# Every second store of the transformed blocks issued from ScalarE's queue instead of SyncE's

## Chip, core and metric

One core of a Trainium2 chip. The metric is the device time of one execution in microseconds, as the median of several runs. Engines are named as in the profile: PE is TensorE (matmuls), PEld its weight loads, DVE is VectorE, ACT is ScalarE, POOL is GpSimd, SP is SyncE. A q behind the name (SPq, ACTq) is the engine's queue, its sequencer.

## What is computed

The kernel computes `x + s * g` for one sequence of L = 2048 rows of D = 512 columns. With `xn` the layer norm of `x`, `g` is a SwiGLU feed-forward of width 1792 with a further silu on its output, and `s` is a state-space convolution with 128 states for each column:

```python
K = jnp.einsum("dn,dnl,dn->dl", Cc, P, dB).real          # P = exp(dt*A*l), l = 0..L-1
Kf = rfft2(pad(K, L)); Uf = rfft2(pad(xn^T, L))
s = irfft2(Uf * Kf)[..., :L]^T + xn * Dskip
g = silu((silu(xn @ w_gate) * (xn @ w_up)) @ w_down)
return x + s * g
```

## The kernel before

The feed-forward is done on TensorE in fp16 with split operands: gate and up halves at line 717 (24 matmuls of 128x256 to a half), down products at line 760 (128x512). The convolution is a transform in stages, written as small f32 matmuls between the feed-forward's. For the convolution kernel K, ACT makes sines and cosines in PSUM (lines 1129 to 1131), DVE multiplies them with amplitudes (lines 1149 to 1157), PE sums over states (line 1181), and `kg_s1` does the first transform stage for 64 columns at a time: matmuls at line 1214 into four PSUM banks, copies out of them by ACT and DVE (line 1221) into a block of 128x2048 floats, an addition of the skip term by DVE (line 1227), and two stores of the block's partition halves, 64 partitions each, to the DRAM array `ak_d` (line 1229). That happens eight times, between 180 and 431 us. Each store moves 512 KB in pieces of 256 bytes.

The second stage (`s2_load`, `s2_prod`, `s2_inv`) loads `ak_d` and the transformed input `ax_d` back (line 464), transforms both (lines 1267 and 1275), multiplies them (DVE at lines 1293 and 1295, POOL at 1297 and 1298), goes back a stage (line 1320, with copies and sums at 1328 to 1330) and stores to `bs_d` (line 1332). `final` loads that and ends with the product with `g` and the sum with `x`.

Nothing waits for an order found while running. Every piece of work is a task, made by `add(engine, planned duration, function, ...)` with the buffers that it reads and writes. A table of numbers, `LIST`, gives the order of all 1989 tasks; each engine does its own in that order. A second table, `PLACES`, gives each SBUF buffer its address in one arena. Both tables are the same before and after. The rest is worked out by `Plan.run`, which goes through the tasks with a clock for each engine and uses the planned times for two things:

- The PSUM banks. When a task first touches a PSUM buffer, it gets the bank that is free earliest by the planned clock (`p0` to `p7`). In the program, a matmul into a bank waits for the bank's last readers.
- Dummy matmuls. `keep_warm` looks for planned gaps on PE. Where they sum to 1.0 us or more within 3.4 us, it fills each with multiplications of a constant by itself (line 1487, 128x512 bf16) into a bank that is free by the plan:

```python
if max(idle(a) for a in (s, s - WARM_SPAN / 2, e - WARM_SPAN)) < WARM_IDLE:
    continue
...
n = int((e - s - 0.2) * WARM_SHARE / WARM_DUR)
```

So a change of a task's engine or planned duration moves no task, but may move banks and dummies behind it. In before, all 35 dummies stand in the first 14 us.

Of the kernel before, what the change touches and what calls it, by code (L numbers as in the profile page):

```python
# [134 lines left out]
class Plan:  # L135
# [19 lines left out]
    def add(self, eng, dur, fn, rd=(), wr=(), up=(), pr=0.0, c=5, dma=0.0, root=False, port=None, f32=0, slack=0.0, ahead=None):  # L155

        t = Task()
        t.eng, t.dur, t.fn, t.pr, t.due, t.root, t.seq, t.dma = eng, dur, fn, (c, pr), pr, root, len(self.tasks), dma
        t.after = None
        t.f32, t.slack, t.ahead = f32, slack, W["ah"] if ahead is None else ahead
        t.port = eng == "POOL" if port is None else port
        deps = set()
        for b in rd:
            deps.update(b.full)
            deps.update(b.part)
        for b in up:  # L170
            deps.update(b.full)
            deps.update(b.reads)
        for b in wr:
            deps.update(b.full)
            deps.update(b.part)
            deps.update(b.reads)
        for b in rd:
            b.reads.append(t)
        for b in up:
            b.part.append(t)  # L180
        for b in wr:
            b.full.append(t)
        t.bufs = list(dict.fromkeys(b for b in (*rd, *wr, *up) if b.kind))
        for b in t.bufs:
            b.left += 1
        t.deps = deps
        t.succ = []
        self.tasks.append(t)
        return t
# [191 lines left out]
def kernel(  # L381
# [7 lines left out]
    nc = tc.nc  # L389
    V, S, G, T = nc.vector, nc.scalar, nc.gpsimd, nc.tensor  # L390
    sy = nc.sync
# [13 lines left out]
    ak_d = dram.tile([32, 2, 64, D], F32, name="ak_d")  # L405
# [37 lines left out]
    add = pl.add  # L443
    bufs = []

    def buf(name, size, group=None, cap=None):
        b = pl.buf(name, size, group, cap)
        bufs.append(b)
        return b

    def bank(name, *kinds):
        b = pl.bank(name, *(kinds or ("p",)))
        bufs.append(b)
        return b
# [3 lines left out]
    def key(name):  # L458
        if name not in K:
            K[name] = pl.key(name)  # L460
        return K[name]
# [522 lines left out]
    def k_target(ch):  # L984
        return W["k0"] + W["ks"] * ch / 8 + bend("bk", ch / D)
# [202 lines left out]
    def kg_s1(i):  # L1188

        pr = k_target(i * 32 + 24)  # L1190
        kp, kh = kps.pop(i)
        khs[i] = kh
        half = lambda t, k: t.rearrange("p (e k b) -> p k b e", k=2, b=32)[:, k]
        lo, hi = (lambda: kh.f32().rearrange("p (k b e) -> p k b e", k=2, e=8)[:, 0]), (lambda: kh.f32().rearrange("p (k b e) -> p k b e", k=2, e=8)[:, 1])

        def even_odd():
            V.tensor_tensor(hi(), lo(), half(kp.t, 1), op=ALU.subtract)
            V.tensor_tensor(lo(), lo(), half(kp.t, 1), op=ALU.add)
        add("ACT", 0.38, lambda: S.copy(lo(), half(kp.t, 0)), rd=[kp], wr=[kh], c=2, pr=pr)
        add("DVE", 0.87, even_odd, rd=[kp], wr=[kh], c=2, pr=pr)  # L1200
        q, s_ = divmod(i, 2)
        if not s_:
            return
        two = [khs.pop(i - 1), khs.pop(i)]
        ka = [bank(f"ka{i}{h}") for h in range(4)]
        b = buf(f"akb{q}", 8192, "akb", int(W["c_akb"] + 0.5))

        def mm():
            for v in range(2):
                for h in range(4):  # L1210
                    u_ = (h // 2 + v) % 2
                    r = slice(h * 32, h * 32 + 32)
                    for k in range(2):
                        T.matmul(ka[h].t[k * 64:k * 64 + 64, u_ * 256:(u_ + 1) * 256], f1k_t[r, k * 64:(k + 1) * 64],  # L1214
                                 two[v].f32()[r, k * 256:(k + 1) * 256], start=True, stop=True, tile_position=(h * 32, k * 64))
        add("PE", 1.0, mm, rd=[*two, key("f1k")], wr=ka, up=[b], c=2, pr=pr, f32=3, slack=1.0)
        for h in range(4):
            def ev(e, h=h):
                o = b.f32().rearrange("p (s u y e j) -> p u y s e j", u=2, y=2, e=8, j=2)
                for u_ in range(2):  # L1220
                    e(o[:, u_, (h // 2 + u_) % 2, :, :, h % 2], ka[h].t[:, u_ * 256:(u_ + 1) * 256].rearrange("p (s e) -> p s e", e=8))
            if h % 2:
                add("DVE", 0.76, lambda ev=ev: ev(V.tensor_copy), rd=[ka[h]], up=[b], c=2, pr=pr)
            else:
                add("ACT", 0.76, lambda ev=ev: ev(S.copy), rd=[ka[h]], up=[b], c=2, pr=pr)
        t0 = lambda: b.f32()[:, 31 * 64:32 * 64]
        add("DVE", 0.2, lambda: V.tensor_tensor(t0(), t0(), dsk[:, q * 64:q * 64 + 64], op=ALU.add), rd=[key(f"dsk{k}") for k in range(2)], wr=[b], c=2, pr=pr, port=True)
        for k in range(2):
            add("SP", 0.52, lambda k=k: sy.dma_start(ak_d.rearrange("g r s d -> (g r) s d")[:, k * 32:k * 32 + 32, q * 64:q * 64 + 64],
                                                     b.f32().rearrange("p (s d) -> p s d", d=64)[k * 64:k * 64 + 64]),  # L1230
                rd=[b], up=[key(f"ak{q // 4}")], c=0, dma=2.8)

# [226 lines left out]
    for pos, (b, c) in enumerate(seq):  # L1459
        while pos >= lead(pos) and 2 * NB * NC - len(downs) < 2 * (pos - lead(pos)) + 2:  # L1460
            d = downs.pop(0)
# [4 lines left out]
    for m in range(D // GT):  # L1466
        kg_tables(m)
        for g in range(m * RT, m * RT + RT):
            kg_trig(g)
            kg_prod(g)  # L1470
            kg_mm(g)
            if g % CB == CB - 1:
                kg_s1(g // CB)
# [61 lines left out]
```

## Time and profile before

| what | value |
|---|---|
| median of 3 runs | 579.1 us (578.53 to 579.45) |
| the profiled execution, its own time | 578.55 us |
| its span, first to last instruction | 576.8 us |
| PE / DVE / ACT / POOL busy | 98% / 76% / 58% / 57% of the span |
| mean granted PE clock | 1.000 |
| share of the DMA engines' time, SP's queue / ACT's queue | 55.5% / 1.5% |

A page of the profile gives busy times, the chain of work that ended last, and groups of equal instructions. A row of a timeline has the start in us, the duration in us, engine, line, operation, `out<-in`, shapes and the count; in brackets stand the idle time of the engine just before it and what ended that. A row of a table by stretch has the stretch, its length, then for PE, PEld, DVE, ACT and POOL the busy time and the count of instructions, then the granted PE clock, the DMA engines' busy share and GB/s. Buffer numbers are left out in rows of the profile: `p` is any PSUM bank, `arena` any SBUF buffer. Which bank is meant is read from the program's order.

### The profile page before, as it was taken

How to read it: one execution, taken by the hardware profiler on the slowest of the kernel's cores; microseconds unless marked ns; L12 is line 12 of the kernel's file. 1: busy time of each engine (PE TensorE's matmuls, PEld its weight loads, DVE VectorE, ACT ScalarE, POOL GpSimd, SP SyncE). 2: the span in 40 equal slices, each digit the busy share in tenths (PEclk: the TensorE clock that was granted, in tenths of full speed). 3: DMA queues.
4: the chain of work that ended last, by engine and by line, in shares of the span. 5: the costliest groups of instructions: out<-in, count | busy, mean ns of one | idle time of the engine just before them, and what ended most of it. 6: DMA issues, size and time to landing. Idle time of an engine off the chain costs nothing.

```text
span 576.8 us, 18270 instructions
## 1 busy us (share of the span) xinstructions
PE 565.2 (98%) x7570; PEld 405.9 (70%) x7570; DVE 440.9 (76%) x1006; ACT 334.7 (58%) x686; POOL 327.1 (57%) x301
## 2 busy tenths in 40 slices
PE   7999999999999999999999999999999999999996
PEld 3788896564886588757867688765766674678765
DVE  5988889846788998988887899977978765643533
ACT  5988667646767266777777778746752323231111
POOL 0144352299998168629998789997516152520041
PEclk9999999999999999999999999999999999999999
DMA  8888722251003171058005452697879987998997
GB/s 249 237 260 265 225 74 74 49 174 67 29 2 85 29 174 47 2 110 275 22 1 126 97 149 74 149 212 181 270 230 248 287 281 218 258 306 234 233 256 203
DMA packets 113155, 93.17 MB, mean 162 GB/s; under 512 B 51184, under 2 KB 97648, under 8 KB 113072
## 3 DMA queue, kind: packets, MB, share of 16 engines
q1 hardware_dynamic: 110432, 89.61, 55.5%
q10 hardware_dynamic: 2640, 2.39, 1.5%
q8 instruction: 59, 0.97, 0.7%
q14 instruction: 24, 0.20, 0.1%
HBM read 55.94 MB, written 32.90 MB: 154 GB/s over the span
## 4 chain that ended last, share of the span: by engine, by line
PE 93%; DMA 2%; SPq 2%; DVE 1%; issue 1%; ACT 0%; DVEq 0%
PE p L717 50%; PE p L760 24%; PE p L1181 5%; PE p L1267 3%; PE p L568 2%; PE p L1275 2%; PE p L1365 2%; PE p L1320 2%; PE p L769 2%; PE p L1214 2%; DMA arena<-bs_d 1%; DMA arena<-in_A_u_dram 1%; SPq L464 1%; PE p L830 1%; SPq L485 1%
## 5 line engine op out<-in xcount | busy, mean ns | idle before, releaser
L717 PE MATMUL p<-arena,wu 128*128 128x256 f16 x1344 | 154.6, 273 | 0.0
L717 PE MATMUL p<-arena,wg 128*128 128x256 f16 x1344 | 154.5, 273 | 0.0
L717 PEld LDWEIGHTS <-wg 128*128 128x128 f16 x1344 | 130.5, 98 | 21.4 <-issue 2.8
L717 PEld LDWEIGHTS <-wu 128*128 128x128 f16 x1344 | 130.2, 98 | 20.2 <-issue 3.7
L760 PE MATMUL p<-wd,arena 128*128 128x512 f16 x630 | 143.2, 379 | 0.0
L760 PEld LDWEIGHTS <-arena 128*128 128x128 f16 x630 | 59.7, 98 | 71.8 <-issue 6.1
L1114 POOL TENSOR_TENSOR arena<-arena 128x1536 f32<-128x1536 f32 x32 | 90.6, 2839 | 22.0 <-DVE arena L850 8.3
L739 ACT ACTIVATE arena<-p,inv 128x512 f32<-128x512 f32 x56 | 37.7, 685 | 65.9 <-PE p L717 62.5
L741 DVE SCALAR_TENSOR_TENSOR p<-p,shc,arena 128x512 f32<-128x512 f32 x56 | 42.0, 756 | 41.9 <-PE p L717 33.3
L1106 POOL TENSOR_TENSOR arena<-arena 128x1024 int32<-128x1024 int32 x32 | 62.4, 1955 | 20.0 <-DVE arena L532 7.8
L743 ACT CAST arena<-p 128x512 f16<-128x512 f32 x56 | 32.6, 586 | 38.4 <-DVE p L741 31.9
L1149 DVE TENSOR_TENSOR arena<-arena,p 128x512 f32<-128x512 f32 x64 | 43.6, 681 | 6.3 <-POOL arena L1047 2.5
L1129 ACT ACTIVATE p<-arena 128x512 f32<-128x512 int32 x64 | 38.5, 606 | 12.9 <-POOL arena L1106 8.3
L1396 POOL TENSOR_TENSOR arena<-arena 128x512 f32<-128x512 f32 x12 | 15.0, 1269 | 49.3 <-DMA arena<-in_A_u_dram 21.6
L1130 ACT ACTIVATE p<-p,halfpi 128x512 f32<-128x512 f32 x64 | 41.9, 662 | 1.2
L744 DVE TENSOR_TENSOR arena<-p,arena 128x512 f16<-128x512 f32 x56 | 37.5, 683 | 6.0 <-ACT arena L743 5.9
L1131 ACT ACTIVATE p<-arena 128x512 f32<-128x512 int32 x64 | 38.0, 604 | 6.9 <-POOL arena L1106 4.2
L1298 POOL TENSOR_TENSOR arena<-arena 128x512 f32<-128x512 f32 x16 | 20.3, 1274 | 30.7 <-DVE arena L1295 26.2
L1297 POOL TENSOR_TENSOR arena<-arena 128x512 f32<-128x512 f32 x16 | 20.4, 1276 | 25.4 <-issue 15.0
L1181 PEld LDWEIGHTS p<-arena 128*32 128x32 f32 x2048 | 29.4, 110 | 5.4 <-issue 2.9
L1181 PE MATMUL p<-arena 128*32 128x64 f32 x2048 | 32.3, 220 | 0.0
L1293 DVE TENSOR_TENSOR arena<-p,arena 128x512 f32<-128x512 f32 x32 | 21.1, 685 | 13.9 <-PE p L1275 7.7
(198 smaller groups left out, 815.5 us busy)
## 6 DMA issues: line engine op xcount, KB each, us to landing
ax_d<-arena SPq DMA_DIRECT2D x32, 256.0 KB, 2.9
ak_d<-arena SPq DMA_DIRECT2D x16, 512.0 KB, 5.6
arena<-ak_d SPq DMA_DIRECT2D x16, 512.0 KB, 4.6
arena<-ax_d SPq DMA_DIRECT2D x16, 512.0 KB, 5.1
bs_d<-arena SPq DMA_DIRECT2D x32, 256.0 KB, 3.8
arena<-in_A_u_dram SPq DMA_DIRECT2D x62, 128.0 KB, 3.9
arena<-in_B_w_down_dram SPq DMA_DIRECT2D x14, 512.0 KB, 5.1
arena<-bs_d SPq DMA_DIRECT2D x12, 512.0 KB, 6.7
```

The source lines that it names most:

```text
L717: T.matmul(pg.t[:, i * 256:(i + 1) * 256].rearrange("p (a t) -> p a t", a=2), w[:, wl, d, i * P:(i + 1) * P], x[:, :, xl, d, :], start=(k ...
L739: add("ACT", 0.69, lambda: S.activation(sg.f32(), pg.t, AF.Silu, scale=inv[:, c, 0:1]), rd=[pg], wr=[sg], c=1, pr=e)
L741: add("DVE", 0.75, lambda: V.scalar_tensor_tensor(pu.t, pu.t, shc[:, c:c + 1], sg.f32(), op0=ALU.mult, op1=ALU.mult), rd=[sg], wr=[pu], c= ...
L744: add("DVE", 0.7, lambda: V.tensor_tensor(hh.view(F16)[:, 512:1024], pu.t, hh.view(F16)[:, 0:512], op=ALU.subtract), rd=[pu], wr=[hh], c=1 ...
L760: T.matmul(z.t, h[:, hl, i * 256 + t * P:i * 256 + (t + 1) * P], w[:, wl, i], start=(c == 0 and i == 0 and k == 0), stop=(c == NC - 1 and ...
L1106: G.tensor_tensor(a, h_[:, :, :, None].to_broadcast([P, 2 * GT, 4, 8]), l_[:, :, None, :].to_broadcast([P, 2 * GT, 4, 8]), op=ALU.add)
L1114: G.tensor_tensor(e, p_[:, :, :, None].to_broadcast([P, 3 * GT, 4, 8]), q_[:, :, None, :].to_broadcast([P, 3 * GT, 4, 8]), op=ALU.mult)
L1129: add("ACT", 0.62, lambda: S.activation(tc_.t, a(), AF.Abs, scale=SIN_SCALE), rd=[an], wr=[tc_], pr=pr)
L1130: add("ACT", 0.7, lambda: S.activation(tc_.t, tc_.t, AF.Sin, bias=halfpi, scale=-1.0), rd=[key("ones")], wr=[tc_], c=4, pr=pr)
L1131: add("ACT", 0.62, lambda: S.activation(ts.t, a(), AF.Sin, scale=SIN_SCALE), rd=[an], wr=[ts], pr=pr + 0.2)
L1149: V.tensor_tensor(o[:, :, 0:64].rearrange("p d (s j) -> p d s j", s=2), e[:, :, 0:64].rearrange("p d (s j) -> p d s j", s=2), t[:, :, None ...
L1181: T.matmul(kt[h * 32:(h + 1) * 32, (r * GD + dd) // 4], o[:, ri, dd + h, 64:96], o[:, ri, dd + h, 0:64], start=(ri == 0), stop=(ri == 1), ...
```

## The change

The second of the two stores, partitions 64 to 127 of the block, is issued by ACT instead of SP. It stays at the same place of `LIST`.

```diff
         for k in range(2):
-            add("SP", 0.52, lambda k=k: sy.dma_start(ak_d.rearrange("g r s d -> (g r) s d")[:, k * 32:k * 32 + 32, q * 64:q * 64 + 64],
+            add(("SP", "ACT")[k], 0.52, lambda k=k: (sy, nc.scalar)[k].dma_start(ak_d.rearrange("g r s d -> (g r) s d")[:, k * 32:k * 32 + 32, q * 64:q * 64 + 64],
                                                      b.f32().rearrange("p (s d) -> p s d", d=64)[k * 64:k * 64 + 64]),
                 rd=[b], up=[key(f"ak{q // 4}")], c=0, dma=2.8)
```

SP's queue has eight issues fewer and ACT's eight more; every other instruction of these two keeps its order. On ACT the eight stand, in order: behind the copy L1199 at 185 us of before's trace; behind two L1130 at 204; behind the first of four copies L573 at 257; behind L1130 at 308; behind L739 at 339; behind the last of four copies L1284 at 390; behind the third of four copies L1330 at 401; behind the cast L743 at 434. POOL's program is the same. On PE and DVE the order of work is the same; banks differ from 197 us on, and ten rows are new on PE. Three places, with the banks' numbers (`p7_106` is bank p7):

PE, between two gate halves L717, which start at 407 us in before's trace. In before the second half follows the first at once. The changed program has these rows, of which five pairs L1487 are new:

```order
L717 MATMUL p1_100<-arena_98,wg_75 128x256
L1487 LDWEIGHTS ones_90
L1487 MATMUL p7_106<-ones_90 128x512
...
L1487 LDWEIGHTS ones_90
L1487 MATMUL p7_106<-ones_90 128x512
L717 LDWEIGHTS wg_75
L717 MATMUL p4_103<-arena_98,wg_75 128x256
```

The planner has come to see a gap there and fills it with five dummy matmuls into p7.

DVE, at 371 to 375 us in before's trace, the products L1149 and L1151 that read the cosines out of a bank; before first:

```order
L1149 TENSOR_TENSOR arena_98<-arena_98,p7_106 128x8x64
L1151 TENSOR_TENSOR arena_98<-arena_98,p7_106 128x8x32
L741 SCALAR_TENSOR_TENSOR p3_102<-p3_102,shc_86,arena_98 128x512
L1149 TENSOR_TENSOR arena_98<-arena_98,p6_105 128x8x64
L1151 TENSOR_TENSOR arena_98<-arena_98,p6_105 128x8x32
```

And the same five rows of the changed program:

```order
L1149 TENSOR_TENSOR arena_98<-arena_98,p3_102 128x8x64
L1151 TENSOR_TENSOR arena_98<-arena_98,p3_102 128x8x32
L741 SCALAR_TENSOR_TENSOR p5_104<-p5_104,shc_86,arena_98 128x512
L1149 TENSOR_TENSOR arena_98<-arena_98,p7_106 128x8x64
L1151 TENSOR_TENSOR arena_98<-arena_98,p7_106 128x8x32
```

The last pair, at 374.04 and 374.64 us, reads p7 instead of p6. The gate half L717 that PE starts at 374.48 us writes p7 in both programs.

DVE and PE, at 440 to 443 us in before's trace: DVE's products of the second stage, and PE's next transform L1267, which alternates between two banks. Before, DVE and then PE:

```order
L1295 TENSOR_TENSOR arena_98<-p5_104,arena_98 128x512
L1293 TENSOR_TENSOR arena_98<-p0_99,arena_98 128x512
L1293 TENSOR_TENSOR arena_98<-p4_103,arena_98 128x512
L1295 TENSOR_TENSOR arena_98<-p1_100,arena_98 128x512
```
```order
L1320 MATMUL p2_101<-arena_98 32x256 x4
L1267 MATMUL p0_99<-arena_98 32x256
L1267 MATMUL p5_104<-arena_98 32x256
```

And in the changed program:

```order
L1295 TENSOR_TENSOR arena_98<-p5_104,arena_98 128x512
L1293 TENSOR_TENSOR arena_98<-p0_99,arena_98 128x512
L1293 TENSOR_TENSOR arena_98<-p4_103,arena_98 128x512
L1295 TENSOR_TENSOR arena_98<-p2_101,arena_98 128x512
```
```order
L1320 MATMUL p1_100<-arena_98 32x256 x4
L1267 MATMUL p0_99<-arena_98 32x256
L1267 MATMUL p2_101<-arena_98 32x256
```

The second bank of L1267 was that of the first L1295, p5; it is that of the last L1295 now, p2.

## The prediction

> **What bounds the kernel now.** I read the page first: busy times, then the chain that ended last.
>
> ```profile
> PE 565.2 (98%) x7570; PEld 405.9 (70%) x7570; DVE 440.9 (76%) x1006; ACT 334.7 (58%) x686; POOL 327.1 (57%) x301
> ...
> PE 93%; DMA 2%; SPq 2%; DVE 1%; issue 1%; ACT 0%; DVEq 0%
> ```
>
> TensorE is busy for 98% of the span and makes 93% of the chain; ScalarE has no visible share of it and SP's queue 2%. Any time that this change is to save or to cost must show on TensorE, as idle time that goes or comes, or as work that is added. Next I looked for TensorE's idle time, with the busy times by stretch (second number of each row: PE busy, of the stretch's length).
>
> ```profile
> 380.00:400.00 20.00, 19.16 (x413) 10.31 (x412) 14.15 (x32) 8.92 (x20) 15.96 (x16) 1.00 0.70 193
> 420.00:430.00 10.00, 8.91 (x355) 5.45 (x354) 6.82 (x14) 5.81 (x14) 1.96 (x2) 1.00 0.69 228
> 440.00:460.00 20.00, 19.81 (x393) 12.32 (x377) 16.84 (x36) 6.97 (x19) 9.39 (x8) 1.00 0.90 277
> 540.00:560.00 20.00, 19.62 (x154) 13.63 (x150) 10.42 (x17) 2.44 (x4) 5.94 (x5) 1.00 0.99 254
> ```
>
> From 20 us to 560 us these four are the only stretches with idle time: 0.84 + 1.09 + 0.19 + 0.38 = 2.50 us. All else there is TensorE running without a break, at a granted clock of 1.00. So at most 2.5 us can be won before the last outputs, and each microsecond put into TensorE's queue, by an instruction or by a wait, is a microsecond of the end.
>
> The stores themselves, from the answer for line 1229 (durations in ns on SP's queue, then issue to landing in us), and the last pair of them in SP's timeline:
>
> ```profile
> L1229 SPq DMA_DIRECT2D ak_d<-arena x16: 580/640/3182, 179.7 to 430.6; - x16
> ...
> DMA to landing us min/median/max: 4.6/5.6/7.6
> ```
> ```profile
> 429.93 3.81 SPq L1229 DMA_DIRECT2D ak_d<-arena  x2
> ```
>
> A first store takes SP about 0.6 us; a second behind it up to 3.18 us.
>
> **The change, part by part.** *SP's queue* loses eight issues of 0.6 to 3.18 us, 5 to 25 us of its time. Its 2% of the chain lies at the end (the chain's last loads), over 100 us behind the last of these stores, and TensorE idles only 0.38 us there. I count the relief as 0; its bound is priced under the rivals.
>
> *ScalarE's queue* gains eight issues. Its DMA instructions hold the queue as SP's do, and none of that form stands on ACT before. The nearest rows are SP's: 0.6 us for a store that stands alone, 3.18 us at most; I take 0.6, since the first store of the pair is in another queue. Whether ACT would wait for the block's data shows at the closest place, the fourth pair: SP could issue from 307.31 us, so the block was ready by then, and ACT's instruction ahead of the new store began at 307.83.
>
> ```profile
> 307.31 2.31 SPq L1229 DMA_DIRECT2D ak_d<-arena  x2
> ```
> ```profile
> 307.83 0.66 ACT L1130 ACTIVATE p<-p,halfpi 128x512 f32<-128x512 f32 x1
> ```
>
> In the other seven ACT comes 0.9 us or more behind SP's first issue, so ACT only pays the issue. Behind the first, second, third, sixth and eighth store ACT next idles by itself:
>
> ```profile
> 187.29 0.60 ACT L1129 ACTIVATE p<-arena 128x512 f32<-128x512 int32 x1 [2.14 <-POOL arena L1106]
> ```
> ```profile
> 207.79 1.12 ACT L1131 ACTIVATE p<-arena 128x512 f32<-128x512 int32 x2 [2.43 <-POOL arena L1106]
> ```
> ```profile
> 260.98 0.58 ACT L838 ACTIVATE arena<-p 128x64 int32<-128x64 f32 x4 [1.29 <-PE p L830]
> ```
> ```profile
> 392.65 0.60 ACT L1131 ACTIVATE p<-arena 128x512 f32<-128x512 int32 x1 [1.78 <-DVE arena L1293]
> ```
> ```profile
> 436.19 0.69 ACT L739 ACTIVATE arena<-p,inv 128x512 f32<-128x512 f32 x1 [1.92 <-PE p L717]
> ```
>
> Each idle time (the number in brackets) is over 0.6 us, so the issue ends in it. The fourth (about 308 us) and fifth (about 340 us) lie in busy stretches of ACT; what stands behind them comes 0.6 us late until ACT's next gap. Since ACT is 58% busy and not on the chain, I count all eight as 0, with the seventh as the risk:
>
> ```profile
> 400.92 0.92 ACT L1330 COPY arena<-p 128x256 f32<-128x256 f32 x3 [0.20 <-PE p L1320]
> ...
> 406.32 0.69 ACT L784 ACTIVATE arena<-p,zsc 128x512 f32<-128x512 f32 x1 [0.75 <-DMA ak_d<-arena]
> ```
>
> Here L784 already waits for the landing of the seventh pair (its output lies where the pair's block lay). The second store now stands behind the three copies L1330, so it is issued at about 401.9 us and lands 4.6 to 7.6 us later, at 406.5 to 409.5: L784 and everything behind it on ACT come 0.2 to 3.2 us late.
>
> *What moves beside it.* The planner counts each second store as time of ACT instead of SP, and from the shifted times it draws other PSUM banks and other gaps to fill. Instruction order is the same otherwise; three things fall on TensorE.
>
> First, five dummy matmuls (line 1487) now stand between two gate halves L717. The trace of before has no gap there:
>
> ```profile
> 407.21 5.40 PE L717 MATMUL p<-arena,wg 128*128 128x256 f16 x48
> ```
> ```profile
> 251.19 5.18 PE p L760 x24
> ```
>
> The 48 matmuls of the two halves run without a break, from 407.21. A matmul of the dummies' size (128x512) costs 5.18/24 = 0.216 us in the second row, from the chain in order of time; five are 1.08 us, with nothing to lie beside. The dummies themselves ran at the kernel's start:
>
> ```profile
> 1.05 7.30 PE L1487 MATMUL p<-ones 128*128 128x512 bf16 x21 [1.05 <-DVE halfpi L470]
> ```
>
> These are 7.30/21 = 0.35 us each, which bounds the term at 1.74 us. I take 1.08: the row in the middle of the stream is nearer to the place.
>
> Second, at 374.48 us a gate half L717 writes bank p7. In before, p7 was free by then; now p7 is the bank that VectorE's L1149 and L1151 read last (p6 in before).
>
> ```profile
> 374.48 1.25 PE L717 MATMUL p<-arena,wg 128*128 128x256 f16 x10
> ```
> ```profile
> 374.04 0.69 DVE L1149 TENSOR_TENSOR arena<-arena,p 128x512 f32<-128x512 f32 x1 [1.13 <-POOL arena L1114]
> 374.64 0.41 DVE L1151 TENSOR_TENSOR arena<-arena,p 128x256 f32<-128x256 f32 x1
> ```
>
> L1151 ends at 375.05, 0.57 us after TensorE was ready; with the hand-over TensorE stands about 0.6 us. L1149 was itself held up by GpSimd's L1114 (the 1.13 in its row), so the term can shrink to 0 if TensorE is later for another reason.
>
> Third, at 441.79 us the transform L1267 alternates between two banks: p0 and p5 in before, p0 and p2 now. TensorE's and VectorE's rows there:
>
> ```profile
> 441.79 1.10 PE L1267 MATMUL p<-arena 64*32 64x256 f32 x32 [0.19 <-DVE arena L1293]
> ```
> ```profile
> 440.45 0.69 DVE L1295 TENSOR_TENSOR arena<-p,arena 128x512 f32<-128x512 f32 x1 [1.13 <-PE p L1275]
> 441.06 1.28 DVE L1293 TENSOR_TENSOR arena<-p,arena 128x512 f32<-128x512 f32 x2
> 442.25 0.68 DVE L1295 TENSOR_TENSOR arena<-p,arena 128x512 f32<-128x512 f32 x1
> ```
>
> VectorE reads p5 with the first L1295 (done 441.14) and the second bank's tenant, p1 in before and p2 now, with the last (done 442.93). The first L1267 matmul starts at 441.79 as before; the second must wait until 442.93 plus a hand-over of 0.05 (L1293 on p0 ended at 441.74, L1267 began at 441.79), so 442.98 instead of 441.85: 1.13 us. VectorE's four instructions were started by TensorE's own L1275, so this wait moves along with TensorE, and earlier delays do not eat it.
>
> Sum: 1.08 + 0.60 + 1.13 = 2.81 us. The profiled execution took 578.55 us (span 576.8, 1.75 around it), so it would take 581.36; the median of the runs shown is 579.1, so I forecast 579.1 + 2.8 = **581.9 us**.
>
> The Trainium skill's page "DMA: Bandwidth & Descriptors", section "Rules for kernel authors", speaks against this change: two transfers of disjoint partition halves share the same 16 engines whichever engine issues them, so spreading them gains no bandwidth and saves only the sequencer's issue time. By that rule alone the sum would be 0 and the time 579.1; it says nothing of banks and dummies.
>
> **The rivals.** *Only the queue changes (0.15).* The bank waits do not come, because TensorE arrives later than in this trace, or the dummies fall into a stall that it has anyway. For it: the second term has a reader that is late for a reason of its own. Against it: the third is tied to TensorE's own time. With the dummies alone the time is 579.1 + 1.08 = 580.2, without them 579.1. The page just named gives the latter; whether the stores gain bandwidth from a second queue, no row of before shows.
>
> *The freed queue wins (0.05).* Faster is possible if spreading the stores takes away TensorE's stalls that the profile puts down to nothing visible. There are two in the chain, the first of them while SP issues the sixth pair:
>
> ```profile
> 384.41 3.52 SPq L1229 DMA_DIRECT2D ak_d<-arena  x2
> ```
> ```profile
> 385.73 0.84 issue
> ...
> 426.03 0.72 issue
> ```
>
> If all 2.50 us of idle time went and neither bank wait came, 1.08 for the dummies would still be added: 579.1 − 1.42 = 577.7. It decides only when at least 2.24 of the 2.50 us go (1.08 + 1.16), since 0.2% is 1.16 us, about what a measurement of this kernel can tell from no change. Against it: 0.56 us of that idle time is TensorE waiting for other engines and not for a queue, the 0.19 of the third term and this:
>
> ```profile
> 424.96 1.07 PE L1214 MATMUL p<-arena,f1k_t 32*64 32x256 f32 x18 [0.37 <-ACT arena L1284]
> ```
>
> *The seventh store holds ACT (0.13).* Where it lands late, L784 and ACT's work behind it are up to 3.2 us late at 406 us. ACT has 0.42 us of idle time next:
>
> ```profile
> 410.86 0.60 ACT L1131 ACTIVATE p<-arena 128x512 f32<-128x512 int32 x1 [0.42 <-POOL arena L1106]
> ```
>
> and the dummies give it 1.08 more. It decides from a landing at about 407.8, 5.9 us after the issue; the median landing is 5.6. At worst TensorE stands 3.2 − 0.42 − 1.08 = 1.7 us more: 581.9 + 1.7 = 583.6.
>
> **How the numbers follow.** The forecast has 0.62, the three rivals 0.15, 0.05 and 0.13; 0.05 is left for other delays on ACT (an issue at 3.18 us instead of 0.6, worst for the third store, which stands inside the four copies L573 at 257 us), which make it slower too. Faster 0.05, same 0.15, slower 0.62 + 0.13 + 0.05 = 0.80. The low end is the dummies alone, 580.2, less 0.2 of the 0.37 that TensorE waits at 424.96, should that wait shrink: 580.0. The high end is 583.6 and one more stall of 0.84: 584.4.
>
> **What would show it.** In the profile after: five L1487 rows near 410 us and no idle time there; an idle of about 0.6 us before L717 near 375 released by DVE L1151; one of about 1.1 us inside L1267 near 444 released by DVE L1295; TensorE's busy time up by about 1.1 us. ACT's DMA rows of 0.6 us show the issue right, rows over 1.5 us show it wrong. The prediction is wrong if the span grows by under 1.2 us, or if more idle time stands at places other than these three.

## The result, and the profile after

| | before | after |
|---|---|---|
| median, 16 runs each | 578.1 us (575.68 to 580.04) | 580.74 us (579.28 to 584.42) |
| profiled execution: time / span | 578.55 / 576.8 us | 581.47 / 579.7 us |

The medians differ by 2.64 us. The ratio of the runs on record is 1.006, with a 95% interval of 1.0046 to 1.0073: slower by 2.7 to 4.2 us. The difference of the medians lies just under that; the other kernels below are priced by the ratio, so this one is too, at 3.5 us. Before's own median is 579.1 us over the three runs of the table further up, and 578.1 over these sixteen.

The page of the changed kernel, busy times and the shares of the chain:

```profile
PE 568.9 (98%) x7575; PEld 406.7 (70%) x7575; DVE 441.0 (76%) x1006; ACT 335.2 (58%) x686; POOL 327.0 (56%) x301
...
PE 94%; DMA 3%; DVE 1%; issue 1%; SPq 0%; POOL 0%; ACT 0%; DVEq 0%; ACTq 0%
```

TensorE is as full as before, with five matmuls more; ACT's queue, which has the moved stores, has 0% of the chain. TensorE's timeline at the three places:

```profile
375.50 2.79 PE L717 MATMUL p<-arena,wg 128*128 128x256 f16 x24 [0.47 <-DVE arena L1151]
...
408.16 2.78 PE L717 MATMUL p<-arena,wg 128*128 128x256 f16 x24
410.78 1.24 PE L1487 MATMUL p<-ones 128*128 128x512 bf16 x5
411.86 2.78 PE L717 MATMUL p<-arena,wg 128*128 128x256 f16 x24
...
443.34 0.62 PE L1267 MATMUL p<-arena 64*32 64x256 f32 x2 [0.19 <-DVE arena L1293]
444.54 1.09 PE L1267 MATMUL p<-arena 64*32 64x256 f32 x30 [0.58 <-DVE arena L1295]
```

Each stands where it was forecast, and both waits name the forecast releaser. VectorE at the first place:

```profile
374.43 0.69 DVE L1149 TENSOR_TENSOR arena<-arena,p 128x512 f32<-128x512 f32 x1 [1.13 <-POOL arena L1114]
375.03 0.41 DVE L1151 TENSOR_TENSOR arena<-arena,p 128x256 f32<-128x256 f32 x1
```

L1151 ends at 375.44 and TensorE goes on at 375.50. The idle time in brackets is too short as a price, because a matmul's end is modelled and a row of two matmuls is drawn 0.62 us long. The price is read from starts: the same matmul in both traces, by how much later it starts in after. Medians of that shift over the matmuls between two places (us):

| behind | start (20 to 370) | 375 | 386 | 410 | 426 | 443 | 472 | 553 |
|---|---|---|---|---|---|---|---|---|
| later by | 0.39 | 1.03 | 0.96 | 2.04 | 1.55 | 2.66 | 3.58 | 3.21 |
| step | | +0.64 | -0.07 | +1.08 | -0.49 | +1.11 | +0.92 | -0.40 |

The three forecast places give 0.64 + 1.08 + 1.11 = 2.83 us. (At 443 itself the step is 1.19; 0.08 of it is gained back by 446.) The others, with a drift of 0.03 between 472 and 553, give 0.39 - 0.07 - 0.49 + 0.92 + 0.03 - 0.40 = 0.38: in this pair of executions they cancel but for the 0.39 of the first 20 us, where the two programs are the same. Behind the last matmul 0.28 is gained back, so that the spans differ by 2.93. Idle time in the stretches, of after (the stretch's length less PE's busy time):

```profile
360.00:380.00 20.00, 19.53 (x376) 14.82 (x374) 18.07 (x45) 16.11 (x35) 18.53 (x16) 1.00 0.67 158
380.00:400.00 20.00, 19.23 (x388) 10.71 (x386) 13.69 (x31) 7.98 (x19) 15.27 (x17) 1.00 0.67 187
420.00:440.00 20.00, 19.80 (x500) 13.88 (x499) 15.46 (x29) 9.31 (x20) 5.06 (x4) 1.00 0.79 226
440.00:460.00 20.00, 19.23 (x399) 11.51 (x398) 15.15 (x32) 6.34 (x18) 9.93 (x8) 1.00 0.89 271
460.00:480.00 20.00, 19.69 (x364) 13.57 (x363) 12.93 (x24) 5.58 (x11) 8.00 (x7) 1.00 0.80 258
540.00:560.00 20.00, 19.70 (x168) 14.31 (x166) 11.16 (x19) 2.88 (x5) 2.74 (x3) 1.00 0.98 238
```

0.47 + 0.77 + 0.20 + 0.77 + 0.31 + 0.30 = 2.82 us. Without the two bank waits (0.47 and 0.58) that is 1.77, and before had 2.50.

The stores (least, median and most in ns on each queue, then issue to landing in us), and ACT around the seventh:

```profile
L1229 SPq DMA_DIRECT2D ak_d<-arena x8: 601/608/652, 180.1 to 431.5; - x8
L1229 ACTq DMA_DIRECT2D ak_d<-arena x8: 582/597/683, 184.1 to 435.3; - x8
...
DMA to landing us min/median/max: 4.4/5.4/8.2
```
```profile
402.00 0.58 ACTq L1229 DMA_DIRECT2D ak_d<-arena  x1
...
407.76 0.69 ACT L784 ACTIVATE arena<-p,zsc 128x512 f32<-128x512 f32 x1 [0.82 <-DMA ak_d<-arena]
409.86 0.60 ACT L1129 ACTIVATE p<-arena 128x512 f32<-128x512 int32 x1 [1.41 <-DVE arena L1151]
```

Every issue takes 0.58 to 0.68 us; the 3.18 that a second store could take on SP is gone. Landings are about what they were (4.6, 5.6 and 7.6 before). L784 waits 0.82 us for the store, 0.75 before, and 1.41 us of idle time behind it swallows what is late. That idle time comes with the plan and not with the store: in experiment 2, where SP issues the store and L784 does not wait, it is 2.28 us, also for L1151.

### The profile page after: what moved, and what is told of

It is laid out like the page before. It is cut to its first block, busy times and chain, and to the rows that moved or that the text cites. A ratio compares the mean times of both kernels' runs of the same rounds, so it can differ in the third digit from the quotient of the medians.

```text
span 579.7 us, 18280 instructions
## 1 busy us (share of the span) xinstructions
PE 568.9 (98%) x7575; PEld 406.7 (70%) x7575; DVE 441.0 (76%) x1006; ACT 335.2 (58%) x686; POOL 327.0 (56%) x301
## 4 chain that ended last, share of the span: by engine, by line
PE 94%; DMA 3%; DVE 1%; issue 1%; SPq 0%; POOL 0%; ACT 0%; DVEq 0%; ACTq 0%
PE p L717 50%; PE p L760 23%; PE p L1181 5%; PE p L1267 3%; PE p L1365 2%; PE p L1275 2%; PE p L568 2%; PE p L1320 2%; PE p L1214 2%; PE p L769 2%; DMA arena<-bs_d 1%; DMA wd<-in_B_w_gate_dram 1%; PE p L1487 1%; PE p L830 1%; POOL arena L1114 0%
## 5 line engine op out<-in xcount | busy, mean ns | idle before, releaser
L717 PE MATMUL p<-arena,wg 128*128 128x256 f16 x1344 | 154.7, 273 | 0.5 <-DVE arena L1151 0.5
L717 PE MATMUL p<-arena,wu 128*128 128x256 f16 x1344 | 154.6, 273 | 0.0
L717 PEld LDWEIGHTS <-wg 128*128 128x128 f16 x1344 | 130.3, 98 | 22.4 <-issue 2.8
L717 PEld LDWEIGHTS <-wu 128*128 128x128 f16 x1344 | 130.2, 98 | 20.3 <-issue 3.3
L760 PE MATMUL p<-wd,arena 128*128 128x512 f16 x630 | 143.2, 380 | 0.0
L760 PEld LDWEIGHTS <-arena 128*128 128x128 f16 x630 | 59.7, 98 | 71.8 <-issue 6.1
L739 ACT ACTIVATE arena<-p,inv 128x512 f32<-128x512 f32 x56 | 37.8, 686 | 66.5 <-PE p L717 63.0
L743 ACT CAST arena<-p 128x512 f16<-128x512 f32 x56 | 32.6, 586 | 39.4 <-DVE p L741 32.7
L1149 DVE TENSOR_TENSOR arena<-arena,p 128x512 f32<-128x512 f32 x64 | 43.6, 681 | 7.4 <-ACT p L1130 3.0
L1130 ACT ACTIVATE p<-p,halfpi 128x512 f32<-128x512 f32 x64 | 41.9, 662 | 1.2
```

Source lines behind the costliest of these rows:

```text
L717: T.matmul(pg.t[:, i * 256:(i + 1) * 256].rearrange("p (a t) -> p a t", a=2), w[:, wl, d, i * P:(i + 1) * P], x[:, :, xl, d, :], start=(k ...
L739: add("ACT", 0.69, lambda: S.activation(sg.f32(), pg.t, AF.Silu, scale=inv[:, c, 0:1]), rd=[pg], wr=[sg], c=1, pr=e)
L760: T.matmul(z.t, h[:, hl, i * 256 + t * P:i * 256 + (t + 1) * P], w[:, wl, i], start=(c == 0 and i == 0 and k == 0), stop=(c == NC - 1 and ...
L1130: add("ACT", 0.7, lambda: S.activation(tc_.t, tc_.t, AF.Sin, bias=halfpi, scale=-1.0), rd=[key("ones")], wr=[tc_], c=4, pr=pr)
L1149: V.tensor_tensor(o[:, :, 0:64].rearrange("p d (s j) -> p d s j", s=2), e[:, :, 0:64].rearrange("p d (s j) -> p d s j", s=2), t[:, :, None ...
```

## The experiments

Theory P is the prediction's: the time is added on TensorE, by what the planner makes of the change (two banks and five dummies), and the queue is worth nothing. Its rivals: Q, the queue costs the time; R, the queue saves and the plan hides it. Prices in us below are ratios to before by the median of before in the same runs (577.0 to 577.5).

**1. The queue alone.** The store is issued by ACT, and the planner does not know it. The lines show the edit against the changed kernel and go on as there.

```diff
-            add(("SP", "ACT")[k], 0.52, lambda k=k: (sy, nc.scalar)[k].dma_start(
+            add("SP", 0.52, lambda k=k: (sy, nc.scalar)[k].dma_start(
```

> The second stores are issued by ScalarE, but the planner still counts them on SyncE, so banks and dummies are those of before. Theory P (the time is added on TensorE by three consequences of the plan: dummies 1.08 us, a bank wait at 375 of 0.6, a bank wait at 443 of 1.13; the queue itself is worth nothing): no change, between -0.6 and +0.6 us against before (ratio 0.999 to 1.001), no L1487 after 20 us, no idle time of TensorE over 0.1 us at 375, and at 443 the 0.19 us of before. Theory Q (ScalarE's work comes later, or the stores in two queues delay other transfers, and that is the cost): +2 to +3.5 us. Theory R (the queue gains and the plan hides it): -0.7 us or lower.

Measured: 1.0002 (0.9990 to 1.0014), +0.1 us (-0.6 to 0.8). TensorE's timeline at the three places, then ACT at the seventh store:

```profile
374.95 2.78 PE L717 MATMUL p<-arena,wg 128*128 128x256 f16 x24
...
407.57 5.40 PE L717 MATMUL p<-arena,wg 128*128 128x256 f16 x48
...
440.88 1.10 PE L1267 MATMUL p<-arena 64*32 64x256 f32 x32 [0.19 <-DVE arena L1293]
```
```profile
407.65 0.69 ACT L784 ACTIVATE arena<-p,zsc 128x512 f32<-128x512 f32 x1 [1.72 <-DMA ak_d<-arena]
```

No wait at 375, no dummies, and the 0.19 of before. Q falls, and R with it as far as 0.6 us can be told.

**2. The plan alone.** SP issues all sixteen stores, and the planner counts as in the changed kernel. Again against the changed kernel, the lines cut short:

```diff
-            add(("SP", "ACT")[k], 0.52, lambda k=k: (sy, nc.scalar)[k].dma_start(
+            add(("SP", "ACT")[k], 0.52, lambda k=k: sy.dma_start(
```

> All sixteen stores are issued by SyncE as in before, but the planner counts the second ones on ScalarE, so TensorE's program is that of the changed kernel, row for row. Theory P: +2.2 to +3.4 us against before, with five L1487 near 410 us, idle of 0.5 to 0.7 us before L717 near 375 and of 1.0 to 1.2 us inside L1267 near 443. Theory Q: -0.6 to +0.6 us. Theory R: +3.5 us or more, over the changed kernel's own.

Measured: 1.0055 (1.0034 to 1.0076), +3.2 us (2.0 to 4.4), with no store on ACT.

```profile
374.85 2.79 PE L717 MATMUL p<-arena,wg 128*128 128x256 f16 x24 [0.47 <-DVE arena L1151]
...
410.07 1.24 PE L1487 MATMUL p<-ones 128*128 128x512 bf16 x5
...
443.54 1.09 PE L1267 MATMUL p<-arena 64*32 64x256 f32 x30 [0.58 <-DVE arena L1295]
```

All three places are there, with the changed kernel's idle times to the hundredth. The plan makes the kernel slower whatever queue the stores are in.

**3. The plan's consequences undone, the queues kept.** Three buffers get their bank by hand, so that neither wait is there: the gate half at 375 us gets p3, the sine that had p3 there p7, and the second bank of L1267 at 443 us is p5. No dummies are added late.

```diff
-                        if owner is None and (best is None or max(x, s) < best[0] - 1e-9):
+                        if owner is None and i == {'ts55': 7, 'pg56': 3, 'pk601': 5}.get(b.name, i) and (best is None or max(x, s) < best[0] - 1e-9):
...
         for s, e, at in gaps:
+            if s > 100:
+                continue
```

> The changed kernel without its five late dummies and with two banks chosen so that neither wait is there (the gate half at 375 us in p3, the second bank of L1267 at 443 us in p5); stores in two queues, planner's clocks as in the changed kernel, all other banks by its own rule. Theory P: -0.6 to +0.8 us against before (0.17 us of idle is left before an L760 at 443 us). Theory Q: still +2 us or more, since the queues are the changed kernel's. Theory R: -0.7 us or lower.

Measured: 0.9992 (0.9979 to 1.0006), -0.5 us (-1.2 to 0.3). TensorE at the three places (line numbers behind 290 are 2 higher):

```profile
373.23 2.78 PE L719 MATMUL p<-arena,wg 128*128 128x256 f16 x24
...
406.40 5.40 PE L719 MATMUL p<-arena,wg 128*128 128x256 f16 x48
...
439.84 1.10 PE L1269 MATMUL p<-arena 64*32 64x256 f32 x32 [0.19 <-DVE arena L1295]
```

With the three gone, the changed queues are as fast as before. It is not shown to be faster.

**4. The bank waits without the dummies.** The last two added lines of experiment 3 alone, with its line numbers.

> The changed kernel without its five late dummies, all else the same. Theory P: +1.3 to +2.1 us against before, 1.08 us under the changed kernel; in the trace the two bank waits at 375 and 443 stay at 0.5 to 0.7 and 1.0 to 1.2 us, since neither depends on the dummies. If instead the dummies gave ScalarE's delayed work time to catch up, about as much idle time as the 1.08 us comes back behind 410 us and the kernel is as slow as the changed one, +2.6 us.

Measured: 1.0017 (1.0001 to 1.0033), +1.0 us.

```profile
374.94 1.26 PE L719 MATMUL p<-arena,wg 128*128 128x256 f16 x10 [0.47 <-DVE arena L1153]
...
407.60 4.64 PE L719 MATMUL p<-arena,wg 128*128 128x256 f16 x41
...
442.20 1.09 PE L1269 MATMUL p<-arena 64*32 64x256 f32 x30 [0.58 <-DVE arena L1297]
```

Both waits stay, and nothing comes back behind 410. The median is below the expected range and the interval reaches into it.

**5 and 6. One bank each.** `{'ts55': 7, 'pg56': 3}` alone, then `{'pk601': 5}` alone.

> The changed kernel with one bank exchanged: the gate half L717 at 375 us writes p3 instead of p7, and the sine that had p3 there takes p7. Theory P: 0.64 us under the changed kernel, +2.0 to +2.4 us against before (ratio 1.0035 to 1.0042); no idle time of TensorE at 375; the five dummies and the wait inside L1267 near 443 as in the changed kernel (the latter 0.9 to 1.15 us from start to start, since its readers are set going by TensorE itself). If the wait only moves on, to the next reader of VectorE behind 375, the 0.47 us of idle time stands at another L717 or L1181 within 10 us and the time is the changed kernel's, +2.8 or more.

> The changed kernel with the second bank of the transform L1267 near 443 us set to p5, as in before, instead of p2; banks behind it go by the planner's own rule. Theory P: 0.96 us under the changed kernel (0.17 us of idle is left before the L760 that follows), +1.6 to +2.1 us against before; in the trace the 32 matmuls of L1267 run without a break behind the first. If the wait only moves on to the products' next bank, 0.5 us or more of idle stands before an L760 or L1275 by 450 us and the time is +2.5 us or more.

Measured: 1.0061 (1.0037 to 1.0085) and 1.0053 (1.0035 to 1.0071), +3.5 and +3.1 us. First the one, then the other:

```profile
374.18 2.02 PE L717 MATMUL p<-arena,wg 128*128 128x256 f16 x17
...
443.33 1.09 PE L1267 MATMUL p<-arena 64*32 64x256 f32 x30 [0.58 <-DVE arena L1295]
```
```profile
427.43 1.08 PE L1214 MATMUL p<-arena,f1k_t 32*64 32x256 f32 x21 [0.47 <-issue]
...
432.84 0.83 PE L717 MATMUL p<-arena,wu 128*128 128x256 f16 x6 [0.52 <-issue]
443.55 1.35 PE L1267 MATMUL p<-arena 64*32 64x256 f32 x32 [0.19 <-DVE arena L1293]
```

In the traces each wait goes and does not move to another bank (at 443 about 0.2 us is left, in front of the L760 that follows). The times do not show it: they are over the terms that are left (1.08 + 1.11 = 2.2 and 0.64 + 1.08 + 0.2 = 1.9 by starts) by 1.3 and 1.2 us, the second just beyond its interval. Something else is in them, and the second trace has idle time put down to nothing visible ("issue") at 427 and 433.

**7. Three times the dummies.** Line numbers behind 300 are 2 higher.

```diff
+            if s > 100:
+                n *= 3
             for i in range(n):
```

> The changed kernel with fifteen dummies at 410 us instead of five. Theory P: each costs its 0.216 us in full, so 2.16 us over the changed kernel, +4.5 to +5.7 us against before (ratio 1.0078 to 1.0099). If TensorE's later work has slack that five dummies did not use up (the late loads at 553, the code that it waits for), it is less: +2.8 to +4.2 us.

Measured: 1.0123 (1.0101 to 1.0146), +7.1 us (5.8 to 8.5), more than either account. The dummies, and a row behind them:

```profile
409.19 3.40 PE L1489 MATMUL p<-ones 128*128 128x512 bf16 x15
...
428.94 1.12 PE L1216 MATMUL p<-arena,f1k_t 32*64 32x256 f32 x31 [1.40 <-issue]
```

By starts the fifteen cost 3.24 us, 0.216 each, as forecast. The rest is again "issue", 1.40 us at 429.

**8. What "issue" is here.** Before, with the 35 early dummies cut in two: the same columns, 70 more rows in TensorE's program.

```diff
-            for i in range(n):
+            for i in range(n * 2):
...
-        return lambda: T.matmul(bank_t[at[0]][at[1]].rearrange("p (a t) -> p a t", a=4), ones,
-                                ones[:, None, :].to_broadcast([P, 4, P]), start=True, stop=True)
+        return lambda: T.matmul(bank_t[at[0]][at[1]].rearrange("p (a t) -> p a t", a=4)[:, :2], ones,
+                                ones[:, None, :].to_broadcast([P, 2, P]), start=True, stop=True)
```

> Before with each of the 35 dummies of the first 14 us cut into two of half the size: the same columns, 70 more instructions in TensorE's program, nothing else. It asks what the idle times put down to issue are (0.84 us at 386 and 0.72 at 426 in before). In the five traces so far each of them stands at a row of TensorE's program whose number is 193 over a multiple of 256, and 59 packets of 16 KB are loaded as code, that is 256 rows of 64 B each. Theory F (TensorE waits there for its next piece of code): the idle times stand again at 193 over a multiple of 256, which are now other instructions, 70 rows earlier in the kernel's work, and none at the old ones (row 9409 is now 9479); the time is within 1.5 us of before to either side. Theory W (the idle time belongs to the instruction, some wait that the profile doesn't show): it stays before the same L1275 at 386 and L1214 at 426, at 0.5 to 0.9 us.

Measured: 1.0045 (1.0020 to 1.0069), +2.6 us, over the 1.5 us expected.

```profile
387.00 1.09 PE L1267 MATMUL p<-arena 64*32 64x256 f32 x30 [1.21 <-issue]
...
424.14 1.52 PE L1267 MATMUL p<-arena 64*32 64x256 f32 x47
427.55 0.83 PE L1267 MATMUL p<-arena 64*32 64x256 f32 x17 [1.89 <-issue]
```

The breaks stand inside other transforms now, but before the same rows of the program, 9409 and 10945, counted in order of start from the trace's rows of TensorE (weight loads, matmuls and its sequencer's own). A third, of 0.75 us at 179 us, stands at row 3521. All three are 193 over a multiple of 256. The forecast of theory F came true: TensorE waits for code. The page of the changed kernel counts its packets:

```profile
q8 instruction: 59, 0.97, 0.7%
```

0.97 MB in 59 packets are 16 KB each, 256 rows if a row takes 64 bytes, and TensorE's program has 15242 rows there, 59.5 x 256.

**9. The dummies' rows without their time.** The five late dummies with 1 column instead of 512.

```diff
-                t.eng, t.start, t.dur, t.bufs, t.fn = "PE", s + i * WARM_DUR, WARM_DUR, [], self.warm(free[-1])
+                t.eng, t.start, t.dur, t.bufs, t.fn = "PE", s + i * WARM_DUR, WARM_DUR, [], self.warm(free[-1], 1 if s > 100 else P)
...
+        return lambda: T.matmul(bank_t[at[0]][at[1]].rearrange("p (a t) -> p a t", a=4)[:, :4 if w == P else 1, :w], ones,
+                                ones[:, None, :w].to_broadcast([P, 4 if w == P else 1, w]), start=True, stop=True)
```

> The changed kernel with its five late dummies cut from 512 columns to 1: their ten instructions stay in TensorE's program, their time nearly goes. It splits what five dummies cost, after fifteen of them had cost 7.1 us against before where 5.0 were expected. Theory T (they cost their own time, 0.216 each): 1.0 us under the changed kernel, +1.4 to +2.2 us against before (ratio 1.0024 to 1.0038). Theory S (a good part of their price is that ten more instructions move the borders at which TensorE loads code, every 256 rows): as slow as the changed kernel, +2.6 us or more, with idle times put down to issue at 426, 432 or 472 as there.

Measured: 1.0062 (1.0042 to 1.0082), +3.6 us (2.4 to 4.7): over theory T's range, in theory S's.

```profile
409.18 0.27 PE L1487 MATMUL p<-ones 128*128 128x1 bf16 x5
...
424.00 1.15 PE L1214 MATMUL p<-arena,f1k_t 32*64 32x256 f32 x11
426.69 1.08 PE L1214 MATMUL p<-arena,f1k_t 32*64 32x256 f32 x21 [1.54 <-issue]
```

The five cost 0.13 us by starts, so 0.95 was saved; in this execution the wait for code at 426 took it back (0.20 in the profiled execution of the changed kernel, at the same row). Row for row, TensorE's program is that of the changed kernel, so such a wait differs between executions too, and one profile of each does not tell how much of it belongs to the program.

**10. The dummies alone.** The changed kernel with the banks of experiment 3 and its dummies.

> The changed kernel with both banks exchanged (p3 at 375, p5 at 443) and the five late dummies left in: the dummies alone. Theory P: 1.08 us for the dummies and 0.17 us of idle before an L760 at 443, so +0.8 to +1.7 us against before (ratio 1.0014 to 1.0029). If the banks are what matters and the dummies lie in a stall that is there anyway, -0.3 to +0.5 us. If the dummies also move the borders of the code to a worse place, +2 us or more, with idle put down to issue of 1.5 us or more in all between 380 and 480 (before 1.56, its copies with the stores in two queues 0.74).

Measured: 1.0036 (1.0019 to 1.0052), +2.1 us (1.1 to 3.0). By the time the last account, by its "issue" of 1.34 us between 380 and 480 not quite; the interval holds the first one's range too. The middle one, that the dummies lie in a stall anyway, falls.

**11 and 12. Other offsets of the code.** Before with the early dummies cut in four and in three: 210 and 140 more rows.

> Before with each of the 35 early dummies cut into four: 210 more instructions on TensorE, which is 46 short of a full piece of code of 256 rows. Theory F: idle put down to issue again only at rows that are 193 over a multiple of 256. Its size at this offset is not known beforehand: with no such idle left between 380 and 480 us the time is 1.6 us below before; with as much as in halves (3.1 us in those two places) it is 1.5 us or more above it.

> Before with each of the 35 early dummies cut into three (128, 128 and 256 columns): 140 more instructions on TensorE. As for quarters: idle put down to issue again only at rows that are 193 over a multiple of 256, and the time goes with its sum, from 1.6 us below before (none left) to 2.6 us above (as in halves).

Measured: 1.0079 (1.0057 to 1.0102), +4.6 us, and 1.0028 (1.0011 to 1.0045), +1.6 us. Of the quarters:

```profile
388.61 0.62 PE L1275 MATMUL p<-arena 32*32 32x256 f32 x4 [1.63 <-issue]
...
430.82 1.93 PE L1267 MATMUL p<-arena 64*32 64x256 f32 x56 [0.74 <-issue]
```

None of the three offsets beats before, and no other version here does. In the fourteen traces the rows of TensorE's timeline put 28 idle times down to issue between 20 and 570 us, and all 28 stand at a row that is 193 over a multiple of 256. Counted by the time between one start and the next, 30 breaks of over 0.5 us stand there, and each ends 1.22 to 1.60 us after a 16 KB packet of code landed. The two series can be paired, one packet to each border: of all about 810 borders in that stretch of the fourteen traces, none was passed sooner than 1.20 us after the landing of its packet, and the 30 breaks stand at that limit. That is what a wait for code looks like.

**All of them together.** The dummies' and the two waits' prices are by starts, as in the table of shifts; "code" is the idle time at those borders in the one profiled execution, less the 0.74 of the queue alone (same TensorE program as before, same time). The choice of that base matters: before's own trace has 1.56 there, and with it every sum would be 0.8 lower. All in us.

| kernel | wait 375 | dummies | wait 443 | code | sum | measured |
|---|---|---|---|---|---|---|
| queue alone | 0 | 0 | 0 | 0 | 0 | +0.1 |
| mended | 0 | 0 | 0.2 | 0.7 | 0.9 | -0.5 |
| no late dummies | 0.64 | 0 | 1.11 | 0 | 1.8 | +1.0 |
| thirds | 0 | 0 | 0 | 1.4 | 1.4 | +1.6 |
| both banks | 0 | 1.08 | 0.2 | 0.6 | 1.9 | +2.1 |
| halves | 0 | 0 | 0 | 3.1 | 3.1 | +2.6 |
| bank at 443 | 0.64 | 1.08 | 0.2 | 0.4 | 2.3 | +3.1 |
| plan alone | 0.64 | 1.08 | 1.11 | 0 | 2.8 | +3.2 |
| bank at 375 | 0 | 1.08 | 1.11 | 0.4 | 2.6 | +3.5 |
| after | 0.64 | 1.08 | 1.11 | 0.5 | 3.4 | +3.5 |
| tiny dummies | 0.64 | 0.13 | 1.11 | 1.8 | 3.7 | +3.6 |
| quarters | 0 | 0 | 0 | 3.8 | 3.8 | +4.6 |
| fifteen dummies | 0.64 | 3.24 | 1.5 | 1.3 | 6.7 | +7.1 |

The sums order the kernels about as the times do, within 1.4 us each; the column "code", from one execution of each, is the least certain.

## Why the prediction was right, point by point

*What bounds the kernel.* Right. The queue alone moves nothing, the plan alone moves TensorE and the time.

*The three terms.* 1.08, 0.60 and 1.13 were forecast; the starts give 1.08, 0.64 and 1.11, and the same steps of 0.64 and 1.08 in every kernel that has the wait or the five dummies. The wait at 375 stayed in all six kernels that have it: in after, as in before, L1149 was held by GpSimd for 1.13 us, so TensorE did not come late enough. The sum was 2.81, the three places give 2.83, the medians 2.64, the ratio 3.5. That the sum is met so closely is in part luck: the other steps between the two traces are up to 0.92 us each and happen to cancel. The time of 581.9 us came out at 580.74, mostly because before's median fell by 1.0 with more runs.

*ACT's queue.* Counted as 0, rightly: experiments 1 and 3. The 0.6 us for an issue was the right end of 0.6 to 3.18. The rule that the prediction weighed, of the Trainium skill's page "DMA: Bandwidth & Descriptors", section "Rules for kernel authors", that a second issuing engine gains no bandwidth and saves only issue time, agrees with the queue alone (ratio 1.0002), though no run here measures the bandwidth by itself. It says nothing of the 3.2 us of the plan alone.

*The seventh store.* It was issued at 402.00 (401.9 forecast) and landed in time for L784 to start at 407.76, just short of the 407.8 from which it would have decided; so small a margin is luck. The bound itself was too strict: in the queue alone L784 starts 6.25 us after the issue, over the 5.9 of the bound, having waited 1.72 us, and the time is still that of before.

*The freed queue wins.* It rested on two idle times put down to nothing visible, one of them while SP issued a store. The plan alone, with SP's issues as in before, has 0.71 us at 386 (0.84 in before, 0.74 with the queue alone). They are waits for code, not for SP.

*What would show it.* Two signs were badly chosen. "An idle of about 1.1 us" inside L1267 is shown as 0.58, and the 0.6 at 375 as 0.47, since the modelled end of the matmul ahead covers the rest. "TensorE's busy time up by about 1.1 us" went up by 3.7: by the 1.08, by such covers, and by the first 20 us, below (0.78). The last sign, that the prediction is wrong "if more idle time stands at places other than these three", does not say more than what. Elsewhere stand 1.58 us, less than the 2.31 of before, but more than the 1.24 that the rows show at the three places.

*What it did not see.* Ten more rows (the dummies' weight loads and matmuls) behind 410 us move the borders of the code there. The six kernels with those ten rows are 0.4 to 1.7 us over the sum of the three terms (+3.2, 3.5, 3.5, 3.1, 2.1 and 3.6 against 2.8, 2.8, 2.2, 1.9, 1.3 and 1.9); the three with the banks or queues of the change and without these rows are 0.8 us under to 0.1 over (+0.1, -0.5 and +1.0 against 0, 0.2 and 1.75). For the changed kernel itself it is 3.5 less 2.8, about 0.7 us that the prediction left out (-0.1 to 1.4 by the ratio's interval, and nothing by the medians), and inside its range. How much of it is code and how much is the scatter of the runs stays open: the offset's effect is shown at the start of the program (experiments 8, 11, 12), not by ten rows at 410 alone with all else as before.

## What to carry to other kernels

Where a planner draws banks and fillers (here the dummy matmuls) from planned times, an edit that costs nothing by itself can move them; give the planner's change and the instruction's change a kernel each before either is blamed. On an engine that is 98% busy, price a wait by the shift of the same instruction's start between two traces, not by the idle time in its row. And where a program streams many short instructions, compare variants of equal length in rows, or expect differences of a few us from the offset alone (1.6 to 4.6 here).

## What the runs showed of the hardware

**Code is a transfer that TensorE can wait for.** Its program comes in 16 KB pieces of 256 rows, and where TensorE gets through one quickly (at 29 of the 30 breaks in 1.8 to 4.6 us without the break; 9.7 is the mean of before's span) it can stand up to 1.9 us at the border. At 27 of the 30 the DMA engines were busy for 0.52 to 0.97 of the time since the border ahead, but at three for 0.02, so loaded DMA engines are not needed for it. Programs 70, 140 and 210 rows longer at the start took 2.6, 1.6 and 4.6 us more. The Trainium skill's page "Runtime: NRT & Kernel Launch", section "Instruction fetch mechanics", gives the 16 KiB and the 256 instructions, and says that the cost of crossing a border is "mostly hidden". The sizes agree, and so does "mostly": at about 780 of the 810 borders one row followed the other within 0.5 us. At the other 30 it took 0.52 to 2.26 us.

**The first 20 us scatter by themselves.** Before and after are the same program there. The row of before, then that of after:

```profile
0.00:20.00 20.00, 16.05 (x93) 7.40 (x94) 13.24 (x53) 13.52 (x23) 0.73 (x5) 1.00 0.95 273
```
```profile
0.00:20.00 20.00, 16.83 (x89) 7.29 (x90) 13.45 (x53) 13.47 (x23) 0.73 (x5) 0.91 0.94 267
```

The granted clock was 1.00 in one and 0.91 in the other. The first gate half started at 18.53 and at 18.90 us. In the eleven traces with this early program it started between 17.07 and 18.99: at 18.81 to 18.99 in the three with a clock of 0.91, at 17.07 to 18.53 in the eight with 1.00. That is a scatter of 1.9 us, of the size of the effects measured here.
